# A two-layer attention and state-space kernel on Trainium2: a fixed issue order for the tables, the last table sums moved to TensorE, and a quarter of a twiddle table generated

## The chip, the cores and the metric

One core of a Trainium2 chip. The metric is device time of the whole program in microseconds (us), lower is better; executions of one kernel mostly lie within 1% of each other. Engines: PE is TensorE, PEld its weight loads, DVE VectorE, ACT ScalarE, POOL GpSimd, SP the engine that issues most transfers.

## The reference, cut to what matters

```python
def _A_ref(x, wqkv, wo):            # attention over 8 keys, 2 positions apart, 32 heads of 16
    ...
def _B_ref(u, A_re, A_im, B_re, B_im, C_re, C_im, log_dt, Dskip):
    dt = jnp.exp(log_dt)[:, None]
    logdA = dt * (A_re + 1j * A_im); dB = dt * (B_re + 1j * B_im)
    P = jnp.exp(logdA[:, :, None] * l[None, None, :])          # 512 channels x 128 states x 2048 lags
    K = jnp.einsum("dn,dnl,dn->dl", Cc, P, dB).real            # the filter
    ...                                                        # y = causal convolution of u with K, by FFT
    return y + u * Dskip

x = A_x                                                        # 2048 positions x 512
x = x + _A_ref(_layernorm(x), A_wqkv, A_wo)
x = x + _B_ref(_layernorm(x), B_A_re, ...)
x = x + _A_ref(_layernorm(x), A_wqkv, A_wo)
x = x + _B_ref(_layernorm(x), B_A_re, ...)
return x
```

The filter K is the same in both layers, so it is made once. The reference rounds the lag numbers to bf16 (a line left out above), so only 641 different lags remain. Each is split into a small and a large step, and K becomes a product of two tables, A (32 small steps) and B (21 large ones), summed over the states on TensorE.

## The kernel before

Table A is doubled level by level: each level multiplies the finished half by two power vectors and adds the two products crosswise (real part, imaginary part). Four tables of 32 columns are made; a column holds the steps of four channels, one from each quarter of the 512. TensorE multiplies each column of A with its column of B in two matmuls (real, imaginary), each with 84 moving columns (21 steps x 4 channels); 8 columns share two banks of PSUM, the memory into which TensorE sums.

```python
def tables(c):
    ...
    for k in range(5):                       # levels of 1, 2, 4, 8, 16
        J = 1 << k
        t2 = tmp(2 * CH * J * 4)
        nc.vector.tensor_tensor(A2[:, :, J:2 * J, :], x, y[0], ALU.mult)
        nc.vector.tensor_tensor(t2..., x, y[1], ALU.mult)
        ...                                  # sw: t2 with real and imaginary part exchanged
        nc.vector.tensor_tensor(o, o, sw, ALU.add)

def products(c):
    for q8 in range(CH // 8):                # a group: 8 columns, two PSUM banks
        pk = psk.tile([P, 2, 512], F32, name="pk")
        for j in range(8):
            ql = q8 * 8 + j
            o = pk[:, j // 4, (j % 4) * NB * 4:(j % 4 + 1) * NB * 4]
            for ri in range(2):
                nc.tensor.matmul(o, lhsT=A[:, ri, ql].rearrange("p i g -> p (i g)"),
                                 rhs=Bt[:, ri, c * CH + ql].rearrange("p b g -> p (b g)"),
                                 start=(ri == 0), stop=(ri == 1))
        nc.scalar.copy(kgs[...], pk[...])    # eviction on ScalarE
    ...                                      # store of the filter rows
```

## Time and profile before

| | before |
|---|---|
| time, median of 3 runs | 543.18 us (542.96 to 544.24) |
| tables end, first q*k products | 131.9 us |
| first row maximum (first softmax) | 151.0 us |
| first matmul of the convolution | 246.4 us |
| mean granted TensorE clock | 0.891 |

Three lines of the profiled execution, besides those that the prediction shows. The first is from the table of busy times (us, share of the span, instructions). The second is a group of instructions: count, then shortest / median / longest duration in ns, and first and last start.

```profile
PE 376.7 (70%) x5272; PEld 277.1 (51%) x5272; DVE 432.6 (80%) x567; ACT 356.9 (66%) x578; POOL 49.8 (9%) x64
```
```profile
L800 PE MATMUL pk<-B_t,A_t x256: 197/201/279, 85.4 to 139.1; 128*128 128x84 bf16 x128
```

TensorE's timeline: start, length, engine, line, operation, output and inputs, weight tile, moving operand, count, and in brackets the idle time before and who ended it.

```profile
102.47 0.76 PE L800 MATMUL pk<-B_t,A_t 128*128 128x84 bf16 x16 [1.57 <-ACT kgs L804]
```

One matmul lasts 201 ns, but 16 take 0.76 us: the next starts while the ones before are still in the array, about 37 ns apart ((0.76 - 0.20) / 15).

### The profile page before, as it was taken

How to read it: one execution, taken by the hardware profiler on the slowest of the kernel's cores; microseconds unless marked ns; L12 is line 12 of the kernel's file. 1: busy time of each engine (PE TensorE's matmuls, PEld its weight loads, DVE VectorE, ACT ScalarE, POOL GpSimd, SP SyncE). 2: the span in 40 equal slices, each digit the busy share in tenths (PEclk: the TensorE clock that was granted, in tenths of full speed). 3: DMA queues.
4: the chain of work that ended last, by engine and by line, in shares of the span. 5: the costliest groups of instructions: out<-in, count | busy, mean ns of one | idle time of the engine just before them, and what ended most of it. 6: DMA issues, size and time to landing. Idle time of an engine off the chain costs nothing.

```text
span 541.9 us, 12380 instructions
## 1 busy us (share of the span) xinstructions
PE 376.7 (70%) x5272; PEld 277.1 (51%) x5272; DVE 432.6 (80%) x567; ACT 356.9 (66%) x578; POOL 49.8 (9%) x64
## 2 busy tenths in 40 slices
PE   2012117446999579988776686599998898796685
PEld 1010014233565377667666585245656676486584
DVE  5988999999499998877678856846989988677853
ACT  5999979967476878857567534375552458587532
POOL 1010101030400000010000002400000022200000
PEclk9999758958999669998888979699998899987889
DMA  8100011121225322018678621100225000369503
GB/s 259 41 1 39 0 77 41 44 59 79 52 67 147 84 70 60 2 42 367 216 224 271 210 79 49 29 0 1 60 74 162 2 1 1 148 247 301 163 1 156
DMA packets 31720, 53.19 MB, mean 98 GB/s; under 512 B 11833, under 2 KB 21178, under 8 KB 30386
## 3 DMA queue, kind: packets, MB, share of 16 engines
q1 hardware_dynamic: 29362, 49.79, 28.0%
q10 hardware_dynamic: 2304, 2.62, 1.4%
q8 instruction: 41, 0.67, 0.5%
q14 instruction: 13, 0.11, 0.1%
HBM read 36.57 MB, written 12.19 MB: 90 GB/s over the span
## 4 chain that ended last, share of the span: by engine, by line
PE 37%; DVE 35%; ACT 13%; DMA 6%; issue 4%; POOL 4%; SPq 1%; DVEq 0%; POOLq 0%; ACTq 0%
PE po L285 6%; PE pq L315 4%; PE pq L132 3%; DVE A_t L781 3%; PE L L244 3%; DVE cm_t L782 3%; PE pp L175 3%; DVE A_t L786 3%; PE pb L611 3%; PE pb L612 3%; DMA kf_dram<-kf_sb 3%; DVE t L596 3%; DVE pav L281 2%; PE pq L298 2%; DVE t L597 2%
## 5 line engine op out<-in xcount | busy, mean ns | idle before, releaser
L241 DVE TENSOR_TENSOR prod<-qT,kT_ext 128x4096 bf16<-128x4096 bf16 x32 | 72.2, 2280 | 10.8 <-PE L L244 7.9
L285 PEld LDWEIGHTS <-pav 128*128 128x128 bf16 x1024 | 64.8, 104 | 17.3 <-DVE pav L281 10.5
L281 DVE TENSOR_TENSOR pav<-attn,v_ext 128x4096 bf16<-128x4096 bf16 x32 | 72.5, 2285 | 1.4 <-DMA v_ext<-v_ext 0.6
L285 PE MATMUL po<-ident,pav 128*128 128x128 bf16 x1024 | 67.9, 229 | 6.0 <-DVE pav L281 6.0
L169 PE MATMUL pt<-ident,xn 128*128 128x128 bf16 x128 | 14.5, 263 | 57.0 <-DVE xn L110 57.0
L611 PE MATMUL pb<-Wp,t 128*128 128x128 bf16 x256 | 37.7, 242 | 19.4 <-DVE t L596 16.7
L175 PE MATMUL pp<-xnT,wqk 128*128 128x512 bf16 x128 | 36.2, 432 | 18.4 <-ACT xnT L171 16.1
L169 PEld LDWEIGHTS <-xn 128*128 128x128 bf16 x128 | 9.6, 114 | 62.2 <-DVE xn L110 60.5
L595 ACT CAST ub<-pb 128x1024 bf16<-128x1024 f32 x32 | 32.1, 1023 | 9.4 <-DVE t L597 8.3
L298 PE MATMUL pq<-wop,oT 128*128 128x512 bf16 x128 | 33.3, 380 | 6.8 <-ACT oT L288 6.8
L570 PE MATMUL pb<-a1s,w_sb 128*128 128x64 bf16 x768 | 31.8, 199 | 8.1 <-ACT kf_sb L550 3.8
L612 PE MATMUL pb<-WpJ,t 128*128 128x128 bf16 x256 | 36.8, 241 | 0.0
L550 ACT CAST a1s<-pb 128x1024 bf16<-128x1024 f32 x30 | 30.2, 1015 | 9.9 <-PE pb L561 8.7
L611 PEld LDWEIGHTS <-t 128*128 128x128 bf16 x256 | 27.8, 110 | 17.4 <-DVE t L596 17.3
L244 PEld LDWEIGHTS <-prod 128*128 128x128 bf16 x1024 | 30.3, 96 | 12.2 <-DVE prod L241 4.8
L570 PEld LDWEIGHTS <-w_sb 128*128 128x128 bf16 x768 | 28.1, 102 | 11.1 <-issue 6.7
L244 PE MATMUL L<-ind,prod 128*128 128x8 bf16 x1024 | 30.9, 166 | 3.6 <-DVE prod L241 3.6
L175 PEld LDWEIGHTS <-wqk 128*128 128x128 bf16 x128 | 13.8, 109 | 37.4 <-issue 28.2
L132 PE MATMUL pq<-xnT,wqk 128*128 128x512 bf16 x128 | 32.6, 394 | 0.0
L315 PE MATMUL pq<-wv,xnT 128*128 128x512 bf16 x128 | 31.3, 378 | 0.4 <-ACT qT L134 0.4
L317 ACT CAST v_ext<-pq 128x512 bf16<-128x512 f32 x32 | 18.3, 587 | 17.8 <-PE pq L315 17.8
L612 PEld LDWEIGHTS <-t 128*128 128x128 bf16 x256 | 27.9, 110 | 4.2 <-issue 3.3
(194 smaller groups left out, 932.6 us busy)
## 6 DMA issues: line engine op xcount, KB each, us to landing
kf_ring<-kf_dram SPq DMA_DIRECT2D x64, 256.0 KB, 4.4
w_sb<-w_dram SPq DMA_DIRECT2D x8, 1024.0 KB, 6.8
kf_dram<-kf_sb SPq DMA_DIRECT2D x16, 256.0 KB, 3.1
v_ext<-v_ext SPq DMA_DIRECT2D x6, 448.0 KB, 3.7
wqk<-in_A_wqkv_dram SPq DMA_DIRECT2D x4, 512.0 KB
x_sb<-in_A_x_dram SPq DMA_DIRECT2D x4, 512.0 KB, 7.7
w_dram<-w_full SPq DMA_DIRECT2D x4, 512.0 KB, 3.8
w_dram<-w_full ACTq DMA_DIRECT2D x4, 512.0 KB
```

The source lines that it names most:

```text
L132: nc.tensor.matmul(pq[:], lhsT=self.wqk[:, dt, ft * P:(ft + 1) * P], rhs=self.xnT[:, dt, q * 512:(q + 1) * 512], start=(dt == 0), stop=(dt ...
L175: nc.tensor.matmul(pp[:], lhsT=self.wqk[:, dt, D + ft * P: D + (ft + 1) * P], rhs=self.xnT[:, dt, b * 512:(b + 1) * 512], start=(dt == 0), ...
L241: nc.vector.tensor_tensor(pr[:], qT[:, ft].unsqueeze(1).to_broadcast([P, W, 4, P]), kap, ALU.mult)
L244: nc.tensor.matmul(L[:, al, w, ft * 8:(ft + 1) * 8], lhsT=pr[:, w, al, :], rhs=ind8[:], start=False, stop=True, skip_group_check=True)
L281: nc.vector.tensor_tensor(pv[:], attn[:, al].unsqueeze(2).to_broadcast([P, W, DH, H]), vap, ALU.mult)
L285: nc.tensor.matmul(po[:, ft, :], lhsT=pvf[:, w, ft * P:(ft + 1) * P], rhs=ident[:], start=(w == 0 and ft == 0), stop=(w == W - 1), skip_gr ...
L298: nc.tensor.matmul(pw[:], lhsT=oT[:, ftp, :], rhs=wo[:, ftp, :], start=False, stop=(ftp == NDT - 1))
L315: nc.tensor.matmul(pp[:], lhsT=xnT[:, dt, a * P:(a + 1) * P], rhs=wv[:, dt, :], start=(dt == 0), stop=(dt == NDT - 1))
L570: nc.tensor.matmul(p2[:, j, :], lhsT=self.w2[:, ec * EC + j, :], rhs=a1s[:, ec * EC + j, :], start=True, stop=True)
L595: nc.scalar.copy(ub[:], p2[:].rearrange("p e q -> p q e"))
L611: nc.tensor.matmul(p3[:, j, :], lhsT=t1[:, dql, :], rhs=wp_r, start=True, stop=False)
L612: nc.tensor.matmul(p3[:, j, :], lhsT=t2[:, dql, :], rhs=wpj_r, start=False, stop=True)
```

## The change

Its intent: take work from VectorE, which is full until 132 us, and from ScalarE, which is full until 64, and order the whole front by hand, so that nothing waits for a scheduler's guess. The core of the diff, cut:

```diff
+    with tc.manual_schedule(engines={ET.DVE, ET.Activation, ET.PE, ET.SP}):
+        k_gen(tc, nc, consts["ident"], ins, kd, la, x_v, lnst, ...)
...
-                nc.vector.tensor_tensor(o, o, sw, ALU.add)
+                if k < 4:                          # the last level is not summed any more
+                    nc.vector.tensor_tensor(o, o, sw, ALU.add)
...
                     for ri in range(2):
-                        nc.tensor.matmul(o, lhsT=A[:, ri, ql]..., rhs=Bt[...], start=(ri == 0), stop=(ri == 1))
+                        nc.tensor.matmul(o, lhsT=A[:, ri, ql]..., rhs=bt,
+                                         start=(ri == 0), stop=False, skip_group_check=True)
+                        nc.tensor.matmul(o[P // 2:P], lhsT=At2[c][:, 1 - ri, ql], rhs=bt,
+                                         start=False, stop=(ri == 1), skip_group_check=True)
...
-    for ch in range(P // ECH):                     # 8 chunks, 4 sines each: the whole second twiddle
-        ...
+    # zero fill of 4 MB, one sine of 128x1024, 16 stores of 64 KB in pieces of 64 B
+    for s in range(4):
+        for j in range(4):
+            nc.sync.dma_start(w2_dram[j::4, s * EQ:(s + 1) * EQ, j * 32:(j + 1) * 32], w2q[s::4])
...
+        for ft, pr in enumerate((spare[:, 0], spare[:, 1], spare2[:])):
+            la.prod(0, ft, pr)                     # three q*k products in freed table buffers
```

The second product of the last level covers only the upper half of the table's 32 steps. So its weights are 64 columns wide instead of 128, and the two forms alternate: full, half, full, half. The twiddle is a table of sines and cosines for the FFT, of which only a quarter is not zero. The rest: norms applied on ScalarE, the loads of the filter and of the residual input and the generation of another table moved behind the products.

## The prediction

> **What bounds the kernel now.** I read four views in this order: the busy table, the stretches of time by engine, the chain of waits, and the timelines of VectorE (DVE) and TensorE (PE). The kernel makes filter tables (0 to 132 us), runs attention (to 246), an FFT convolution, then both again. The change touches the first 246 us. The stretches (start and end, length, busy us of PE, weight load, DVE, ScalarE (ACT), GpSimd, then granted clock and DMA) show who limits which stage:
> ```profile
> 14.90:35.30 20.40, 0.00 (x0) 0.00 (x0) 19.09 (x36) 20.26 (x40) 2.20 (x3) 1.00 0.02 6
> 35.30:64.30 29.00, 7.93 (x32) 3.39 (x32) 25.64 (x48) 28.73 (x54) 0.39 (x1) 0.96 0.04 18
> 99.40:114.70 15.30, 2.90 (x64) 2.56 (x64) 15.13 (x21) 10.76 (x25) 5.54 (x3) 0.73 0.17 46
> 131.80:190.40 58.60, 50.49 (x714) 30.16 (x714) 48.51 (x40) 37.25 (x53) 8.00 (x4) 0.88 0.32 83
> 190.40:246.00 55.60, 49.35 (x590) 38.56 (x591) 46.86 (x51) 42.07 (x88) 5.20 (x9) 0.93 0.18 57
> ```
> Until 64 us ACT is full and DVE nearly so. From 64 to 132 DVE makes the four A tables and is full; ACT has room. After 132 PE leads.
>
> The chain shows how the setup starts late: ACT waits for a fourth copied input before it may load its sine table.
> ```profile
> 10.34 0.62 PE pt L687 x4
> 10.99 0.59 ACT in_C_im L716
> 11.59 1.28 ACT L704
> ...
> 14.88 0.69 DVE sq_z L709
> ```
> DVE's timeline shows the other two things that matter: three passes per table level (two multiplies, one sum), and a hole after the tables.
> ```profile
> 124.14 2.29 DVE L781 TENSOR_TENSOR A_t<-A_t,pow_t 128x4096 bf16<-128x4096 bf16 x1
> ...
> 129.49 2.28 DVE L786 TENSOR_TENSOR A_t<-A_t,cm_t 128x4096 bf16<-128x4096 bf16 x1
> 131.88 4.50 DVE L241 TENSOR_TENSOR prod<-qT,kT_ext 128x4096 bf16<-128x4096 bf16 x2
> 142.99 2.29 DVE L241 TENSOR_TENSOR prod<-qT,kT_ext 128x4096 bf16<-128x4096 bf16 x1 [6.62 <-PE L L244]
> ```
> PE's timeline explains the hole: it must finish table products and query projections before it can consume the first products q*k and free their two buffers.
> ```profile
> 131.83 2.07 PE L800 MATMUL pk<-B_t,A_t 128*128 128x84 bf16 x27 [3.75 <-DVE A_t L786]
> 133.70 3.57 PE L132 MATMUL pq<-xnT,wqk 128*128 128x512 bf16 x8
> ...
> 141.95 0.94 PE L244 MATMUL L<-ind,prod 128*128 128x8 bf16 x32
> ```
>
> **What the Trainium skill says.** "TensorE: Matmul & The Clock Gate", Part 1, says a cold array issues a matmul of N columns every N / 1.2 GHz and a warm one every N / 2.4 GHz plus about 2.5 ns: for 84 columns, 70 and 37.5 ns. The trace agrees: 27 in 2.07 us above (about 70 apart after taking off one latency), and elsewhere 32 in 1.38 us (about 37). "ScalarE: Activation LUTs", What ACT_TABLE_LOAD costs, gives about 2.7 us with the drain; here the load itself takes 1.28 us. "DMA: Bandwidth & Descriptors", Measured, gives about 10.5 ns per packet as a floor; no transfer of 64 B pieces is in this trace, so I use that figure as an estimate below.
>
> **The change, part by part.**
>
> *Last sums to PE.* Each of four tables loses its widest sum, 2.20 us from start to start: 8.8 us of DVE. PE gets two more matmuls for each of 128 columns, 256 x 37.5 ns = 9.6 us warm, 18 cold, spread over four groups of 128 matmuls (4.8 us each warm instead of 2.4).
>
> *Second twiddle.* Three quarters of it is zeros. Before, 32 sines (eight groups of four, 2.9 us a group) and 16 index passes at about 0.53 us cost ACT 32 us, and eight masks cost DVE 8 x 0.34 = 2.7 us. After: one sine of 1024 wide (about 1 us), two passes (1.2) and one mask (0.7). The zeros are one 4 MB fill; the quarter goes out in 16 transfers of 1024 pieces of 64 B. Their tile's memory is then reused by the A tables: in the built program the first table write waits for all 16. Estimate: 16384 pieces / 16 engines x 10.5 ns = 11 us, or 16 issues at 0.6 us (48 kernel stores here show a median of 598 ns) = 10 us, plus a landing of 2.4 us as for those stores. Issued at about 44, they end near 57; the tables start near 62. So hidden, but with only some 5 us to spare.
>
> *Norm applies and issue order.* Twelve of 16 applies (0.33 us each) go from DVE to ACT: DVE -4.0, ACT +6. The seed copies go the other way: DVE +0.8. Sum for DVE up to the tables' end: -8.8 - 2.0 - 4.0 + 0.8 + 0.6 (last level split in eight) = -13.4 us.
>
> *Start.* The sine load comes before the input copies. DVE however must now do its constants first, which wait for a small ACT copy. I get first squaring at 13.1 instead of 15.6: -2.5.
>
> *Squaring loop.* Per step ACT has 0.96 (square) + 0.94 + 0.53 + 0.51 (copies) = 2.94 us and DVE 2.4 to 2.9, so ACT leads: two steps of 2.9, one of 1.9, five of 2.94 from 13.1 end at 35.5; the twiddle step takes 4.3, two more end near 45. DVE then still has 16 us of B tables: 61 to 62, against 64.25 before.
>
> *Tables.* One table is now 12.1 us (14.5 measured for the last, less 2.2 and the seed's start). But the fixed order ties them to ACT. Before table 0's last level DVE needs the second block's statistics: ACT does 4 applies (2.2), two transposed copies (1.9), four key copies paced by a cold PE (about 5), eight statistics at 0.72 (5.8), reaching 72.8 where DVE is at 69.5: wait 3.3. Tables 0 and 1 end at 77.5 and 90.2. ACT then puts block 3's statistics (93.7 to 99.5) ahead of the product evictions, so PE with its two output banks stands still, then runs products, query projection, block 2, products, block 3 in line: key copies of block 2 at 114.2, of block 3 at 126.2. DVE ends the tables at 119.9 and waits until 126.3 for the last.
>
> *First attention.* Three q*k products now have buffers of their own (the freed table space), so the hole goes, but the fourth waits for PE to end the last table products (about 132). I get the first row maximum, which was at 151.0, at 138.8: -12.2. Without the ACT and PE waits of the last paragraph it would be 133: -18.
>
> *Rest of the first attention.* From the first row maximum to the end it took 246.4 - 151.0 = 95.4 us; in layer 2, with no filter loads or generated table in it, 473.5 - 381.8 = 91.7. The change moves both of those behind the products: two to four switches between the exponential and sine tables (1.28 us each) leave the chain, and the 2.65 us transfer of values before the first weighted sum goes from it. Against that the last stage gets 3.6 us of filter permutes and about 4 us of generated table more on ACT, which was 42.07 of 55.6 busy: about 50 now, no longer slack. I take 94: -1.4.
>
> Sum: -12.2 - 1.4 = -13.6; with half the distance to the freer case (-18 and -1.4 is -19.4), -16. 543.2 - 16 = 527.
>
> **The rivals.** (a) *DVE alone decides.* All of the -13.4, the earlier start and the hole (7.9 us of waits) come through, and layer 1's attention runs like layer 2's: about -20 to -24, 520. For it: DVE is 15.13 of 15.30 busy at the tables, and the order was clearly laid out by hand. Against: the statistics and evictions above. (b) *The small writes hold the tables.* If a 64 B piece costs 20 ns rather than 10.5, the 16 transfers take 21 us, end at 67 and cost 5 us: 532. At 40 ns the gain is gone: 540 or more. For it: nothing here shows such pieces. Against: a kernel store of 256 pieces of 128 B lands in 2.4 us (the view of transfers). (c) *The strict order makes ACT or PE the bound.* PE falls to half clock in each gap (granted clock was 0.73 in the third stretch above), doubled products take 9 us cold instead of 4.8, and everything behind them stands in line: 532 to 537. (d) *Filter loads come too late.* They now start behind the products; if the second half's permute stands in ACT's queue before its data, 2 to 5 us come back. The chain already had such a wait, 3.42 us.
>
> **Range and chances.** (a) pulls to 520, (b) to (d) to 532 and above; I take 527 with 518 to 536 for 8 in 10. Faster by 2% means below 532.3: 0.78. Within 2%: 0.20. Slower: 0.02.
>
> **What would show it.** The first table write near 62 us with no wait on a transfer in front of it; a wait of DVE for ACT's statistics in table 0; the last level without its sum; the last key copies near 126 and DVE idle before them; three products in a row, then the first row maximum near 139; the first attention ending near 231 instead of 246; everything after it unchanged in length. Wrong if DVE waits long for the small writes, if the row maximum comes before 134 or after 144, or if the stage after the products grows by more than 4 us.

## More of the kernel before

With the inputs of this case K is small: it moves the output little.

## The result, and the profile after

The changed kernel takes 601.38 us (median of 4; 599.59 to 603.3) against 543.07 us of the kernel before beside it (median of 4). A ratio is the mean time of one kernel's fast runs over that of the other's of the same rounds, so not quite the ratio of the medians: 1.107, 95% interval 1.103 to 1.112. It is 11% slower. The prediction was wrong, in direction too: it gave "slower" a chance of 0.02.

The table of busy times of the changed kernel, then the groups of the two forms of table matmul:

```profile
PE 458.4 (76%) x5490; PEld 325.9 (54%) x5528; DVE 417.7 (70%) x554; ACT 335.3 (56%) x537; POOL 36.2 (6%) x56
```
```profile
L909 PE MATMUL pk<-B_t,A_t x256: 201/253/254, 76.1 to 200.5; 128*128 128x84 bf16 x128
L911 PE MATMUL pk<-B_t,A_t x256: 225/277/281, 78.1 to 200.7; 128*64 128x84 bf16 x128
```

VectorE and ScalarE lost work as planned (432.6 to 417.7 us and 356.9 to 335.3). TensorE gained 82 us of busy time, from 376.7 to 458.4, for 256 more matmuls. Their durations, 253 and 277 ns at the median, are close to the 201 ns of before and give nothing away. The timeline does. The same 84-column matmuls, one by one:

```profile
78.11 0.28 PE L911 MATMUL pk<-B_t,A_t 128*64 128x84 bf16 x1 [1.82 <-DVE A_t L876]
78.32 0.25 PE L909 MATMUL pk<-B_t,A_t 128*128 128x84 bf16 x1
78.50 0.28 PE L911 MATMUL pk<-B_t,A_t 128*64 128x84 bf16 x1
78.72 0.25 PE L909 MATMUL pk<-B_t,A_t 128*128 128x84 bf16 x1
```

They start 0.21, 0.18, 0.22 us apart, 0.197 on average over a group: most of a duration, five times the 37 ns of before and nearly three times the 70 ns of a row at half clock (experiment e7 below). They hardly overlap. The weight loads of the same moments (TensorE's weight-load timeline) show a second thing:

```profile
78.32 0.10 PEld L909 LDWEIGHTS <-A_t 128*128 128x128 bf16 x1
78.50 0.13 PEld L911 LDWEIGHTS <-A_t 128*64 128x64 bf16 x1
```

Each load starts together with its own matmul (78.32 and 78.50 above). In a row of one width it starts a matmul earlier: in e7 the weights of the matmul of 78.59 are loaded at 78.52. So in alternation no weights are loaded ahead.

A group of 32 takes 6.3 us at half clock, 12 of the 16 groups. Together the 512 keep TensorE busy for 98 us (14.5 before). TensorE's stretches of time (start and end, length, then busy us of PE, weight load, DVE, ACT, GpSimd, granted clock, share of the DMA engines, GB/s) show what that does:

```profile
78.00:104.00 26.00, 25.89 (x136) 15.65 (x137) 14.15 (x27) 7.14 (x12) 2.35 (x3) 0.50 0.00 1
104.00:150.00 46.00, 44.07 (x235) 24.94 (x234) 26.22 (x42) 22.36 (x41) 1.27 (x2) 0.69 0.09 19
150.00:209.20 59.20, 57.73 (x402) 34.47 (x405) 13.03 (x10) 13.84 (x21) 1.14 (x2) 0.59 0.05 12
```

From 78 to 209 us TensorE is the bound, while DVE, full in this stage before, idles more than half of it. The granted clock stays at 0.50 over 26 us in which PE counts as busy for 25.89 (the ends of matmuls are modelled, so busy is not the same as working). And DVE's timeline names whom it waits for:

```profile
103.00 0.24 DVE L866 COPY A_t<-c_t 128x256 bf16<-128x256 bf16 x1 [10.53 <-PE pk L909]
175.35 0.69 DVE L208 COPY kT_ext<-kT_ext 128x2032 bf16<-128x2032 bf16 x1 [24.74 <-ACT kT_ext L202]
209.16 1.22 DVE L281 TENSOR_REDUCE mx<-L 128x128 bf16<-128x1024 f32 x1 [1.64 <-PE L L248]
```

The third and fourth table cannot start until PE has read the first and second (two buffers); the fourth waits another 14.10 us at 133.09. The last keys come 24.7 us late because their matmuls stand behind table products in PE's fixed order. The first row maximum comes at 209.2 us, which was at 151.0 before and predicted at 138.8. The rest of the program is as long as before: from there to the convolution's first matmul (305.3) 96.1 us against 95.4, and from that to the end 295.1 against 295.5.

### The profile page after: what moved, and what is told of

The parts are those of the page before. It is cut to its first block, busy times and chain, and to the rows that moved or that the text cites. A ratio compares the mean times of both kernels' runs of the same rounds, so it can differ in the third digit from the quotient of the medians.

```text
span 600.4 us, 12789 instructions
## 1 busy us (share of the span) xinstructions
PE 458.4 (76%) x5490; PEld 325.9 (54%) x5528; DVE 417.7 (70%) x554; ACT 335.3 (56%) x537; POOL 36.2 (6%) x56
## 4 chain that ended last, share of the span: by engine, by line
PE 52%; ACT 18%; DVE 17%; DMA 5%; issue 4%; POOL 2%; SPq 1%; POOLq 0%; DVEq 0%; ACTq 0%
PE pk L911 9%; PE pk L909 8%; PE pp L199 5%; PE pq L345 4%; PE po L315 4%; PE pq L145 4%; PE L L248 3%; DVE pav L311 3%; PE pb L647 3%; PE pb L648 3%; PE pb L597 2%; DMA kf_dram<-kf_sb 2%; DVE t L633 2%; DVE t L632 2%; ACT xnT L192 2%
## 5 line engine op out<-in xcount | busy, mean ns | idle before, releaser
L911 PE MATMUL pk<-B_t,A_t 128*64 128x84 bf16 x256 | 69.5, 272 | 1.8 <-DVE A_t L876 1.8
L909 PE MATMUL pk<-B_t,A_t 128*128 128x84 bf16 x256 | 63.4, 248 | 9.1 <-POOL ln_rstd L102 9.1
L245 DVE TENSOR_TENSOR prod<-qT,kT_ext 128x4096 bf16<-128x4096 bf16 x29 | 65.6, 2281 | 3.7 <-ACT qT L147 2.7
L914 ACT CAST kgs<-pk 128x672 bf16<-128x672 f32 x16 | 11.5, 718 | 76.1 <-PE pk L911 76.1
L911 PEld LDWEIGHTS <-A_t 128*64 128x64 bf16 x256 | 32.1, 125 | 22.2 <-DVE A_t L876 2.0
L909 PEld LDWEIGHTS <-A_t 128*128 128x128 bf16 x256 | 26.4, 103 | 29.4 <-POOL ln_rstd L102 9.6
L190 PE MATMUL pt<-ident,x_blk 128*128 128x128 bf16 x64 | 7.3, 288 | 41.4 <-ACT x_blk L120 41.4
L328 PE MATMUL pq<-wop,oT 128*128 128x512 bf16 x111 | 29.7, 380 | 11.3 <-ACT oT L318 10.1
L647 PEld LDWEIGHTS <-t 128*128 128x128 bf16 x256 | 27.5, 109 | 17.1 <-DVE t L632 17.0
L318 ACT CAST oT<-po 128x512 bf16<-128x512 f32 x32 | 18.5, 579 | 25.2 <-PE po L315 25.2
```

What stands on the lines that cost most here:

```text
L245: nc.vector.tensor_tensor(pr, self.qT[q][:, ft].unsqueeze(1).to_broadcast([P, W, 4, P]), kap, ALU.mult)
L647: nc.tensor.matmul(p3[:, j, :], lhsT=t1[:, dql, :], rhs=wp_r, start=True, stop=False)
L911: nc.tensor.matmul(o[P // 2:P], lhsT=At2[c][:, 1 - ri, ql], rhs=bt, start=False, stop=(ri == 1), skip_group_check=True)
```

## The experiments

Eighteen kernels were run, each beside the kernel before on the same chip: 4 executions each (6 for e9 and e11 to e19), but for the two tests of values, which have one. They ran on three chips, so compare ratios rather than times between rounds. The letter e and a number is a run's name; there is no run e10 on record. Line numbers in the fences differ a little between kernels, and the diffs are cut and shortened: full(...) and half(...) stand for the matmul of full and of half width. The table has the changed kernel and the nine that carry the argument.

| run | time, us | ratio to before (95%) | start to start in a group (cold: at half clock) | first row maximum |
|---|---|---|---|---|
| changed kernel | 601.38 | 1.107 (1.103 to 1.112) | 197 ns, cold | 209.2 |
| e2 pairs | 565.20 | 1.044 (1.039 to 1.048) | 265 ns a pair, cold | 177.9 |
| e1 grouped (wrong sums) | 532.32 | 0.985 (0.979 to 0.990) | 44 to 78 ns | 140.6 |
| e3 all half-width | 533.79 | 0.986 (0.982 to 0.990) | 47 ns, cold | 139.0 |
| e7 padded to full width | 533.23 | 0.985 (0.981 to 0.989) | 70 ns, cold | 141.1 |
| e14 grouped, one start per bank | 533.88 | 0.983 (0.980 to 0.985) | 44 to 78 ns | 140.6 |
| e4 sum back on VectorE | 531.99 | 0.981 (0.975 to 0.987) | no half-width form | 140.6 |
| e19 as e4, residual load earlier | 530.44 | 0.978 (0.973 to 0.983) | no half-width form | 139.4 |
| e5 alternating sums in the kernel before | 615.39 | 1.134 (1.128 to 1.140) | as changed kernel | 222.6 |
| e6 grouped sums in the kernel before (wrong sums) | 544.71 | 1.001 (0.994 to 1.008) | as e1 | 151.7 |

### Is it the change of form?

The theory: each change between the 128-wide and the 64-wide form drains the array, that is, the next matmul waits until the one before has left it. The Trainium skill says so of a change of tiling mode in "TensorEngine Tiling (Array Packing)", Tiling Modes, Key Properties: "Changing tiling mode (not just tile) drains the TensorE". It gives no number. Rivals: the half-width form itself is slow; adding onto the same PSUM columns waits; the fixed order and the late loads cost, and the clock merely makes the products look long. Four kernels separate these.

**e1**, the 16 full-width matmuls of a group first, then the 16 of half width:

```diff
-                for j in range(8):
-                    for ri in range(2):
-                        full(j, ri); half(j, ri)
+                for j in range(8):
+                    full(j, 0, True, False); full(j, 1, False, True)
+                for j in range(8):
+                    half(j, 0, False); half(j, 1, True)
```

> Changed kernel, only the order of the 32 table matmuls of a PSUM bank pair (8 columns): first the 16 of full width, then the 16 of half width; same count, same data. Theory S (each change between the 128-wide and the 64-wide form drains the array, so that the next matmul starts about 0.197 us later instead of 37 to 70 ns): 2 changes per group instead of 32, so a group takes 1.5 to 2.8 us instead of 6.29, the four tables' products lose about 60 to 75 us of PE, and the time falls to 520 to 535. Rival W (the half-width form itself is slow, by its weight load): 16 x 0.2 + 16 x 0.05 = about 4 us a group, time 550 to 575. Rival O (the fixed order and the late loads are what costs, the products only look long because the clock is cold): within 10 us of 601.

Measured: 532.32 us. Same 512 matmuls, same operands, 69 us less than the changed kernel.

**e2**, per column two full-width, then two half-width ones: half as many changes of form.

```diff
+                for j in range(8):
+                    full(j, 0, True, False); full(j, 1, False, True)
+                    half(j, 0, False); half(j, 1, True)
```

> Changed kernel, per column the two full-width matmuls, then the two half-width ones: half as many changes of form (16 of 32 starts in a group). Theory S: cost goes by changes: 16 x 0.197 + 16 x 0.05 = about 4.0 us a group, time about midway between the grouped version and the changed kernel, 555 to 570. Rival W: slow half-width form costs the same in any order; then this and the grouped version take the same time.

Measured: 565.2 us, about midway (the middle of 532.3 and 601.4 is 566.9). TensorE's timeline of e2; the view joins each pair into one row:

```profile
78.01 0.32 PE L907 MATMUL pk<-B_t,A_t 128*128 128x84 bf16 x2
78.26 0.35 PE L913 MATMUL pk<-B_t,A_t 128*64 128x84 bf16 x2
78.54 0.32 PE L907 MATMUL pk<-B_t,A_t 128*128 128x84 bf16 x2
```

A pair starts every 0.265 us (0.25 and 0.28 in turn): 0.197 for the change and 0.07 for the second of a pair, which overlaps at the cold rate. The cost goes by changes, not by matmuls.

**e3**, every full-width matmul split into two of half width, so that all 48 of a group are of half width:

```diff
-                        nc.tensor.matmul(o, lhsT=lw, rhs=bt, ...)
+                        nc.tensor.matmul(o[0:P // 2], lhsT=lw[:, 0:P // 2], rhs=bt, start=(ri == 0), stop=(ri == 1), ...)
+                        nc.tensor.matmul(o[P // 2:P], lhsT=lw[:, P // 2:P], rhs=bt, start=(ri == 0), stop=False, ...)
```

> Changed kernel, every full-width table matmul split into two of half width (lower and upper 64 outputs), so six half-width matmuls per column, 48 a group, and no change of form within a group. Theory S: 48 starts at 37 to 70 ns, 1.8 to 3.4 us a group, although there are half as many matmuls again; time 522 to 545. Rival W (half-width is slow in itself): 48 x 0.2 = 9.6 us a group, time over 650. Rival A (accumulating onto the same PSUM columns right after the matmul before is what waits): the order of accumulation is as in the changed kernel, so about 6 us or more a group, time about 600.

Measured: 533.79 us. TensorE's timeline of e3:

```profile
77.81 0.28 PE L914 MATMUL pk<-B_t,A_t 128*64 128x84 bf16 x1
77.88 0.27 PE L912 MATMUL pk<-B_t,A_t 128*64 128x84 bf16 x1
77.89 0.28 PE L910 MATMUL pk<-B_t,A_t 128*64 128x84 bf16 x1
77.95 0.28 PE L914 MATMUL pk<-B_t,A_t 128*64 128x84 bf16 x1
```

Half again as many matmuls, and no loss: the half-width form is not slow. L910 writes the lower 64 outputs, L912 and L914 the upper ones, and two starts fall on one moment (77.88 and 77.89): the two halves of the array run side by side, three matmuls in the 0.14 us from one L914 to the next.

**e7**, the second products padded with 64 zero columns, so that all matmuls are full-width ones in the old alternating order (one padded tile; two early q*k products instead of three for want of memory):

```diff
+        t2p = tabz.tile([P, 2 * CH, P], BF16, name="A_t2p")
+        nc.gpsimd.memset(t2p[:, :, 0:P // 2], 0.0)
-                        nc.tensor.matmul(o[P // 2:P], lhsT=At2[c][:, 1 - ri, ql], ...)    # 64 wide
+                        nc.tensor.matmul(o, lhsT=At2[c][:, 1 - ri, ql], ...)              # 128 wide
```

> Changed kernel with the last level's second product written into a tile of twice the width whose lower 64 columns are zero, so that all four matmuls of a column are full-width ones, in the same alternating order; the smaller levels' second products sit in the table's unused upper half, the padded tile is single, and only two (not three) of the early q*k products have a buffer of their own. Theory S: no change of form at all: 32 starts at 37 to 70 ns, 1.2 to 2.3 us a group, time 518 to 535. Rival A (accumulation onto the same columns waits): order and targets are unchanged, so about 6.3 us a group and about 600. Rival O: about 600.

Measured: 533.23 us. TensorE's timeline of e7:

```profile
78.52 0.28 PE L910 MATMUL pk<-B_t,A_t 128*128 128x84 bf16 x1
78.59 0.28 PE L912 MATMUL pk<-B_t,A_t2p 128*128 128x84 bf16 x1
```

Order, targets and number of matmuls are those of the changed kernel, only the width differs: 70 ns apart instead of 197. So it is not the adding onto the same columns. And since e1, e3 and e7 keep the fixed order and the late loads, it is not those. What is left is the change of width. What happens inside a change is not shown: TensorE may wait until the array is empty, as the page has it, or only for weights that are not loaded ahead (the two load lines above). Both go with the change of width, and no run separates them.

### The part alone, in the kernel before

**e5** puts only the alternating sums into the kernel before; **e6** the same grouped as in e1.

```diff
+                if k == 4:
+                    At2[c] = t2...            # second products kept, no sum
+                    continue
                 nc.vector.tensor_tensor(o, o, sw, ALU.add)
```

> Kernel before with one part of the change alone: the last level's sum left out on VectorE and made on TensorE by alternating full and half-width matmuls (the second products of the last level sit in the scratch buffers, those of the smaller levels in the table's unused upper half). Theory S: 4 x (25 - 3 to 5) = 80 to 88 us more of TensorE in the table stage, of which its idle half hides some 30 to 40; time 575 to 600. Rival O: the sums are harmless without the fixed order: 533 to 545.

Measured: 615.39 us, worse than I expected and worse than the changed kernel. Its DVE waits for the one scratch buffer, which the second products of the table before still hold (the changed kernel has two such buffers, so part of the excess is my version's); the first of these waits:

```profile
110.03 2.29 DVE L782 TENSOR_TENSOR cm_t<-A_t,pow_t 128x4096 bf16<-128x4096 bf16 x1 [18.30 <-PE pk L805]
```

So the sums on TensorE, alone, carry a loss of this size without the fixed order.

> As the run before it, with the matmuls grouped (16 of full width, then 16 of half width). Theory S: VectorE's tables lose 8.8 us, TensorE's products take 6 to 11 us in place of 2.4 to 5 per table but lie beside VectorE except for the last; time 533 to 541, against 542 of the kernel before. If the gain is under 2 us, the time after the tables is set by TensorE and ScalarE there, not by VectorE.

Measured: 544.71 us, ratio 1.001. VectorE's 8.8 us do not come through here: it waits 2.84 us for keys, 2.73 us for a scratch buffer and 6.95 us for table products after the last table, and the first row maximum stays at 151.7.

### Are the sums of the grouped version right?

The output of e1 passed the comparison with the reference, but a filter this small hardly shows in it. The Trainium skill gave cause for doubt: "PSUM — Partial Sum Buffer", The four PSUM rules, says that a second matmul marked as start in a bank makes the next matmul of a group still open there overwrite instead of add, without an error. In e1 the columns 1 to 3 of a bank are started while column 0 still waits for its half-width sums. **e15** makes each group twice, as in e1 and column by column as in e2, and adds 1000 times the difference to the filter. **e16** does the same test on a version in which only a bank's first matmul is a start. **e14** is that version without the test.

```diff
-                    full(j, 0, True, False)
+                    full(j, 0, j % 4 == 0, False)        # e14: one start per bank
...
+                nc.vector.tensor_tensor(k2[:], kg, k2[:], ALU.subtract)                          # e15, e16
+                nc.vector.scalar_tensor_tensor(kg, k2[:], 1000.0, kg, ALU.mult, ALU.add)
```

> Test of values, not of time: each group is made twice, as in the first grouped version and column by column in the same order of adding, and 1000 times the difference is added to the filter. If a later start in the bank makes the half-width sums overwrite, the result is incorrect; if the sums are the same, it is correct.

> The same test on the version with one start per bank: the differences should all be zero, result correct, whatever the outcome of the test before.

> Grouped version in which only the first matmul of each bank is marked as a start; all others add, or overwrite where nothing has been written since. Same matmuls in the same order. Theory S: 528 to 535, as the grouped version (532.3); the mark costs no time. If grouping were fast only because of wrong sums, 560 or more.

Measured: e15 incorrect, relative error 2.66; e16 correct. So the grouping of e1 makes wrong sums that the ordinary comparison let pass, as the page says, and the mark cures it. The same grouping is in e6, e8, e9, e11 and e12, whose sums must be taken as wrong too; their times stand, as kernels they are not to be used. (The two tests take 621 and 615 us in one run each, which says nothing.) e14, with the same matmuls in the same order, takes 533.88 us. Its timeline once the clock is up:

```profile
82.34 0.76 PE L907 MATMUL pk<-B_t,A_t 128*128 128x84 bf16 x16 [1.03 <-ACT kgs L923]
83.04 0.79 PE L913 MATMUL pk<-B_t,A_t 128*64 128x84 bf16 x16
```

16 in 0.76 us, the same row as in the kernel before. From the first row's start to the second's it is 0.70 us where 16 pipelined starts take 0.60, so one change costs about 0.1 us at this clock. Grouping keeps its time with right sums.

### What the sums on TensorE are worth

**e4** keeps the whole change, but makes the last sum on VectorE again.

```diff
-                if k < 4:
+                if True:
                     nc.vector.tensor_tensor(o, o, sw, ALU.add)
```

> Changed kernel with the last level's sum back on VectorE and only the two full-width matmuls per column on TensorE; everything else of the change stays (fixed order, quarter twiddle, norms on ScalarE, early products). Theory S: no change of form, so the 600 us are gone: 530 to 539. Against the grouped version it adds 4 x 2.2 = 8.8 us to VectorE's tables, but there VectorE stands idle 5.9 us for the last keys anyway, so the difference should be about 3 us, not 8.8. Rival O (fixed order costs): still near 600.

Measured: 531.99 us; e14 has 533.88 in other rounds, and the ratios to the kernel before, 0.981 and 0.983, lie within each other's intervals. I expected 3 us of loss; none shows. The stretch of time from 120 to 152 us, in e4:

```profile
120.00:152.00 32.00, 27.61 (x396) 18.10 (x395) 30.97 (x22) 16.32 (x26) 1.13 (x2) 0.89 0.15 33
```

and in e14:

```profile
120.00:152.00 32.00, 30.28 (x490) 20.14 (x489) 23.48 (x19) 18.69 (x28) 1.14 (x2) 1.00 0.15 30
```

With the sum on VectorE, DVE is busy 30.97 of 32 us and PE 27.61; with the sum on TensorE, PE is busy 30.28 and DVE 23.48. The sums moved the bound from one engine to the other. Both versions reach the first row maximum at 140.6 and the second at 151.3 and 151.8.

### Where the other microseconds are

The versions without the loss take 532 to 534, not 527. In e1 two waits of DVE were left, 5.92 us for the last keys (as predicted) and 4.34 us at the start of the convolution for the store of the generated table. DVE's timeline of e1:

```profile
127.08 0.69 DVE L208 COPY kT_ext<-kT_ext 128x2032 bf16<-128x2032 bf16 x1 [5.92 <-ACT kT_ext L202]
```

**e8** puts ScalarE's statistics of the last block behind the evictions and the query projection behind the last keys; **e11** also gives the fourth early product a buffer; **e9** makes the generated table one block of weighted sums earlier; **e12** is e11 and e9 together; **e13** is e4 with four early products and e9's edit.

```diff
-        stats(3, "act"); products(1); la.front_q(0); front(2)        # e8
+        products(1); front(2); stats(3, "act")
...
+        la.front_q(0)                                                # after front(3)
-        for ft, pr in enumerate((spare[:, 0], spare[:, 1], spare2[:])):        # e11
+        for ft, pr in enumerate((spare[:, 0], spare[:, 1], spare2[:], pr3[:])):
-                        fill(); fill()                               # e9
+                        fill(); fill(); fill()
```

> Grouped version with another fixed order: the evictions of the second table's products and the second-last key block ahead of the last block's statistics on ScalarE, the query projection after the last key block. Theory L (the remaining 5 us to the prediction lie in VectorE's wait for the last keys, 5.9 us in the grouped version, made by ScalarE's statistics standing ahead of the evictions): wait under 1.5 us, first row maximum at about 135 instead of 140.6, time 524 to 529. Rival (what is behind the products sets the end anyway, its late filter loads and generated table): first row maximum moves, the time does not, 530 to 533.

Measured: 533.56 us, just above the rival's range. DVE's wait for keys fell from 5.92 to 1.55 us, but the first row maximum came at 140.2: TensorE's line behind it took its place.

> The reordered version (533.6, first row maximum at 140.2 although VectorE's wait fell from 5.9 to 1.6 us) with the fourth early product also given a buffer of its own, so that its 32 matmuls stand ahead of the next query projection on TensorE. Theory Q (TensorE's line after the tables sets the first row maximum: 3.6 projection, 5.7 table products, 2.6 sums of products, 5.3 next projection, 0.9): the maximum comes at 135 to 136, and the time falls to 526 to 530 if nothing later takes it back. Rival: ScalarE's evictions or the rest of the attention set it; the maximum moves, the time stays at 531 to 535.

Measured: 535.36 us, again just above the rival's range. DVE's timeline of e11:

```profile
135.58 1.22 DVE L281 TENSOR_REDUCE mx<-L 128x128 bf16<-128x1024 f32 x1 [1.46 <-PE L L248]
```

The first row maximum moved to 135.6 as worked out, the second stayed at 151.9 (151.8 in e1). PE is busy 31.33 of the 32 us from 120 to 152 there, as in e8. The row maximum was my marker for the end of the stage, and it no longer sets the time. TensorE's sum of table products and projections of queries and values probably does; that is argued from its busy time and not tested.

> Grouped version with three instead of two steps of the second generated table per weighted sum, so that its last sine is done one block of sums earlier. In the grouped version VectorE and ScalarE wait 4.34 and 3.48 us at the start of the convolution for the last store of that table, whose memory they reuse. Theory T (that wait is a real loss of the change, about 3 us): wait gone, time 528 to 531. Rival: ScalarE has no room earlier and the sums lengthen by as much; within 1.5 us of the grouped version, 531 to 534.

Measured: 533.03 us; the wait at the start of the convolution only fell to 3.63 us.

> Both of the two before: fourth early product and the generated table finished earlier. If both theories hold, the gains add: 523 to 527. If the chain behind the first row maximum is set by TensorE and ScalarE alone, 530 to 534.

Measured: 537.43 us. That is above even the rival's 530 to 534: the ratio, 0.990 (0.988 to 0.993), lies clear of e14's, so the edits together cost time.

> The version with the last sum back on VectorE (532.0), with four early products in table buffers (those of the second products are free at once there) and the generated table finished earlier. First row maximum about 138 to 139 instead of 140.6, no wait for a store at the start of the convolution; 526 to 530. If it ends with the twelfth kernel, making sums on TensorE is worth nothing even when grouped.

Measured: 533.63 us (median of the five fast runs; one of six was slow; ratio 0.982), above the range. The first row maximum came at 137.7, and the second at 152.7. The wait for the store did not go: 3.62 us are left.

The chain of waits of e14 has two transfers in the rest of the attention that the change had moved there (start, length, what):

```profile
168.37 5.92 DMA x_sb<-in_A_x_dram
239.64 3.28 DMA g_dram<-g_s
```

**e17** issues the load of the residual input before the third query projection in e14, **e18** adds e9's edit, **e19** does e17's edit in e4.

```diff
+            for b in range(4):
+                x_load(b)
             qproj(2)
...
             qproj(3)
             linit(3)
-            for b in range(4):
-                x_load(b)
```

> Grouped with one start per bank, and the four loads of the residual input issued before the third query projection instead of after the fourth. Theory D (the 5.92 us transfer that stands on the chain at 168 to 174 us is a real loss): the weighted sums start 2 to 5 us earlier, time 529 to 532. Rival F (TensorE's full line up to 166 us sets the weighted sums anyway): 533 to 535.

Measured: 535.58 us (532.15 to 539.66). The load left the chain, the time stayed. But the edit did more than move the load. Outside the tables the order of issue is not fixed by hand, and it changed: the fourth row maximum came at 177.6 instead of 188.7, ahead of the weighted sums, which started at 183.0 instead of 176.7, later and not 2 to 5 us earlier. The convolution's first matmul came at 244.5 instead of 237.6, and what follows it took 285.9 us instead of 295.1. So e17 is no clean test of the load, and a marker that moves by 7 us can leave the time as it is.

> The same, and three instead of two steps of the generated table per weighted sum. Theory D: the 3.28 us store leaves the chain too: 526 to 530. Rival F: 532 to 535.

Measured: 533.00 us, with the same new order. The store left the chain too and the time stayed, as the rival said.

> Sum on VectorE as in the kernel before, rest of the change, residual loads earlier. Theory D: 526 to 530 (from 532.0); rival F: 531 to 534.

Measured: 530.44 us, ratio 0.978 (0.973 to 0.983). The median is a little above the range that I gave, and 1.5 us below e4's in other rounds. It has the lowest median, with right sums, and beats both kernels: 2.2% under the one before by ratio, with an interval from 1.7 to 2.7%. Its interval overlaps e4's, and the order of issue changed here as in e17.

## Why the prediction was wrong, point by point

**Last sums to PE: the failed step.** It said "256 x 37.5 ns = 9.6 us warm, 18 cold, spread over four groups of 128 matmuls (4.8 us each warm instead of 2.4)". The count was right, the rate was not: it was taken from a row of matmuls that all have one form. In alternation all 512, the old ones too, start 197 ns apart at half clock, where most of them ran, so four tables of products take 98 us instead of 19 (512 x 37 ns). The mechanism that I left out is the wait at each change of width, which the page calls a drain; e2 shows that it goes by the number of changes, e3 that the narrow form is quick on its own, e7 that the order of adding is innocent. The page of the skill that states it was in reach and I did not open it, because the operation was "a matmul" to me and not "a matmul of another width". The first row maximum is 70.4 us behind the predicted one (209.2 - 138.8), and the total 74.4 behind (601.4 - 527).

**Rival (c)** named TensorE as the bound, but priced it at a cold clock, "9 us cold instead of 4.8". It was the right engine with the wrong size: 25 us for a table.

**Start, squaring, small writes, norms: right.** DVE's first squaring started at 13.5 (predicted 13.1); before it was at 16.1 and not at 15.6, so the gain of 2.5 us came as predicted. The wait for the statistics in table 0 was 2.70 + 0.59 = 3.3 us (predicted 3.3). The 16 small stores took 11.55 us to issue and landed 3.1 us after (predicted 10 to 11 and 2.4), and the first table write came at 62.0 with no wait before it:

```profile
61.98 0.24 DVE L866 COPY A_t<-c_t 128x256 bf16<-128x256 bf16 x1
```

So rival (b) fell, and the second twiddle's quarter did what it should. The price of a piece was in part luck: the page gives 10.5 ns for a small transfer as a whole, and I used it for each of the 16 engines.

**Tables and first attention: right once the drain is gone.** e14 and e1, which have the change without its alternation, end the wait for the last keys at 127.1 (predicted 126.3), after 5.9 us of idle time (predicted 6.4), and reach the first row maximum at 140.6 (predicted 138.8). What I drew from it was too much: e11 brought the maximum 5 us forward for no gain in time. And the sum of -8.8 us on VectorE brings no time that shows here (e4); TensorE, busy for 30.28 of the 32 us from 120 to 152 in e14, is the likely reason.

**Rest of the first attention: off by 3 us.** I took 94 us, -1.4 against before, and leaned on 91.7 us for layer 2. That was a misreading: 473.5 is in no view, the first matmul of the second convolution is at 475.2, and the stage takes 93.4. e14 needs 97.0 from the first row maximum to the convolution's first matmul (237.6 - 140.6). Two transfers left the chain as I said, and two others stand on it now, 5.92 and 3.28 us. That these are the missing microseconds was only partly borne out: e17 and e18 moved them and gained nothing, e19 gained 1.5 us, which is inside the scatter, and all three changed the order of issue as well. What exactly holds the versions at 530 to 534 stays open; the runs show that it is neither the wait for the last keys (e8) nor the first row maximum (e11).

## What to carry to other kernels

Before a matmul is put between others, compare the widths of their weights: a change of width here cost 0.1 us with the clock up (e14) and 0.13 us at half clock (197 - 70 ns), each time, and a duration in the profile doesn't show it; the distance between starts does. Group by width or pad to one width, and mark only one start in a bank if groups stay open side by side. When a bound engine's work is moved to another one, look at how full that one is behind the stage, and test values with a difference that is enlarged, not only with the final output.

## What the Trainium skill lacked or had wrong

- "TensorEngine Tiling (Array Packing)" says that a change of mode drains, without a number. Here, with 84 columns, starts are 197 ns apart in full alternation between 128 and 64 wide weights, against 70 ns at the same half clock without a change; with the clock up one change costs about 0.1 us. The page also does not say that no weights are loaded ahead across a change, as the load lines of the changed kernel show.
- The same page says that tiles run in parallel, without a measured number for two 64-wide halves. e3 shows 47 ns a matmul, against 70 of a full-width one at the same cold clock. Its note that column tiling turns the fast weight load off fits the 128 ns against 104 at the median for one weight load in the changed kernel; in e3 the narrow loads cost nothing.
- "TensorE: Matmul & The Clock Gate", Part 1, has the clock come up after about 3.4 us of sustained work. In the changed kernel it stayed at 0.50 for 26 us in which the records show PE busy for 25.89: alternation does not seem to count as sustained work. In e2, with half the changes, it is 0.60 in the same stretch; in e4, without half-width matmuls, 0.63 with PE busy for only 14.15. No run separates the alternation from other causes.
- "DMA: Bandwidth & Descriptors" has about 10.5 ns per packet as a floor, from a small load as a whole, and no measured cost of 64 B stores. Here 16 stores of 1024 such pieces were issued in 11.55 us, 11.3 ns a piece for each of 16 engines, which were busy 80% of the time from 46.8 to 59.1 us. The rate of issue may have set the pace as much as the pieces.
